# Attention's front end with q and k transposed together, and the first two network parts on their own

## The chip, the cores and the metric

The kernel runs on one core of a Trainium2 chip. The metric is the device time of one execution in microseconds (us); the times of the kernel before are 451.82 us in the median of three runs, from 448.97 to 453.68. Five engines work side by side, each through its own list of instructions in a fixed order: PE (TensorE), DVE (VectorE), ACT (ScalarE), POOL (GpSimd) and SP (SyncE, which here only issues transfers). PEld is PE's loading of weights, which overlaps its matmuls.

## The reference

Three computations follow each other. `x` goes from one to the next, and the result is 768 by 512.

```python
q_bucket = np.sum((q @ proj > 0) * 2 ** np.arange(6), axis=-1)   # k_bucket likewise
scores = np.where(q_bucket[..., :, None] == k_bucket[..., None, :], (q @ k.T) / 8, -1e9)
x = softmax(scores) @ v                # 8 heads, 768 rows, 64 columns per head
idx = np.argmax(x @ w_gate, axis=1)    # 8 experts, 192 slots each, rows beyond them give 0
x = prob[idx] * (relu(x @ w1[idx]) @ w2[idx])          # w1 512x1024, w2 1024x512
h = x @ w_in                           # w_in 512x2048, w_out 2048x512
out = (h * np.tanh(softplus(h))) @ w_out
```

## The kernel before, in words

**Attention.** Rows come in six tiles of 128 (NT). Each head loads q, k and v from three tensors (`ldq`, `ldk`, `ldv`, L593, 192 KB each). So that PE can work on them in fast form, each number is split into a rounded part and what is left of it (hi and lo; `qh kh vh`, L607 to L611, and `ql kl vl`, L619). The hi and lo columns of a row tile lie side by side, so one transpose turns both: 12 transposes per head in four units of three (`t1`, L625), each unit copied out of PSUM by ACT or DVE (`e1`, L630 to L636). 12 matmuls give the hash of each row (`hash`, L653, 12 output columns), and three DVE operations make the bucket number (`bits`, L658, L660, L664). DVE then writes two one-hot blocks of 64 columns, one for q and one for k (`noh`, `oh`, L669). Another 12 transposes turn them together with the lo columns (`t2`, L625), and four more copies take them out (`e2`). Each row tile's scores are four matmuls of 384 columns (L692, L694), in which the one-hot rows add a large negative number wherever the buckets differ. Then come the row maximum (DVE, L700), the exponential (ACT, L708), the transposes of the result (L722), its split (ACT L727, DVE L732), the product with v (L744), its copy out (`ao`), a product that stacks the heads and makes routing logits (`comb`, L755), and the division (L760 to L773). For head 0 the front end stands alone; for each later one it lies between the pieces of the head ahead of it.

**Weights.** They come as float64 in 512 KB pieces into a ring of raw tiles (`wd`, SP, L543). DVE makes them float32 (L552, L554, L559), ACT rounds them (`wh`, L573), and DVE or POOL takes what is left (`wl`, L580). While attention runs, 13 chunks and the zeroing of the slot table (`slots<-zt`, L823) are already issued by SP.

**Experts.** Rows are scattered into the slot table, and each of eight experts does its two products (L1064, L1106) with turns between them. The lo part of the hidden rows is `mhl` (DVE, L1100), the lo part of the result `x2l` (L1145).

**Network.** 16 parts f. Part f has 24 matmuls of 384 columns (L1232), copies `hs` (ACT, L1242), then the activation: `em` (DVE L1249), exponential `e1` (ACT L1252), logarithm `ln` (ACT L1255), `u` (DVE L1258), sigmoid `sg` (ACT L1261), `hm` (DVE L1264), and the split `gh` (ACT L1269), `gl` (DVE L1272). The second product has 18 matmuls of 512 columns per part (L1278). ACT loads a table of functions whenever it goes from one function to the other, and parts are taken in pairs for that: `ln` of an f waits for `e1` of both, `sg` for `u` of both.

**The order.** A planner (class `Planner`) writes every engine's list. It takes tasks with durations, needs and buffers (`attention_tasks`, `expert_tasks`, `network_tasks`), always picks the one that can start earliest (in steps of 0.03 us), and breaks ties by a number per task (`WHEN`, `FIRST` for head 0, `THEN` behind attention). At run time every engine waits for the next instruction of its list.

Of the kernel before, what the change touches and what calls it, by code (L numbers as in the profile page):

```python
# [27 lines left out]
WHEN = dict(idr=142.35, pw=-4386.57, hq=1487.71, wg=-2258.33, ldq=-1065.41, ldk=408.14, ldv=-933.74, qh=4350.55,  # L28
            kh=7076.95, vh=-2343.1, ql=-1970, kl=-1005.3, vl=-1974.29, t1=328.97, e1=-3068.68, hash=-2989.07,
            bits=-3218.52, noh=-1694.11, oh=67.94, t2=-4179.97, e2=-727.14, sc=444.63, max=-637.61, exp=454.86,  # L30
            at=-500.47, hi=-164.99, lo=-592.17, av=548.75, ao=2666.7, iw=93.96, comb=-1492.56, rd=335.58,
            xn=-1105.92, xx=-1665.2, lm=-2664.42, wd=46.84, wh=1211.43, wl=-766.44)
FIRST = dict(idr=-652.1, pw=3097.94, hq=-5268.81, wg=4852.97, ldq=-3302.54, ldk=-4013.68, ldv=-2005.56,
             qh=-1840.12, kh=-619.74, vh=-193.5, ql=674.23, kl=1694.78, vl=1753.74, t1=514.73, e1=-4820.19,
             hash=-1040.76, bits=-3757.41, noh=1020.62, oh=1163.2, t2=-335.62, e2=-12.95, sc=-671.62,
             max=-449.07, exp=-3416.38, at=-1894.24, hi=-3265.28, lo=-59.9, av=55.37, ao=-2910.58, iw=6221.07,
             comb=660.11, rd=2707.9, xn=396.72, xx=-575.46, wd=2263.3, wh=-1337.27, wl=291.71)
# [17 lines left out]

class Task:
# [1269 lines left out]
```

## Time and profile before

| | |
|---|---|
| profiled execution | 450.76 us, of which the span is 449.0 us |
| PE, PEld | 418.1 us (93%), 373.2 us (83%) |
| DVE, ACT, POOL | 348.4 us (78%), 322.8 us (72%), 85.9 us (19%) |
| to the first score matmul | 15.55 us |
| attention to the last stacking product | 137.05 us |
| routing and scatter | 27.40 us |
| experts | 119.50 us |
| network | 144.20 us |

The stages are cut where PE goes over from one to the next, and lie one behind the other. The granted clock is TensorE's, 1.00 being 2.4 GHz and 0.50 being 1.2 GHz. A matmul's own duration overlaps that of the next one, so the distance between starts says what one costs.

### The profile page before, as it was taken

What the parts mean: (1) busy time and instruction counts of PE and PEld (TensorE: products, weight loads), DVE (VectorE), ACT (ScalarE), POOL (GpSimd) and SP (SyncE); (2) the same over time, 40 slices, a digit from 0 to 9 for tenths busy, and PEclk for the clock granted to TensorE, in tenths of its full rate; (3) what the DMA queues carried; (4) which work ended last, traced back from release to release, by engine and by line L of the source; (5) the groups of instructions that cost most, each with busy time, mean ns of one, the idle gap of its engine ahead of it and who ended that gap; (6) DMA issues with size and microseconds to landing.
All of it is one profiled execution on the core that took longest, in us unless ns stands there. A gap on an engine that the chain in (4) does not pass through costs nothing.

```text
span 449.0 us, 7298 instructions
## 1 busy us (share of the span) xinstructions
PE 418.1 (93%) x2630; PEld 373.2 (83%) x2630; DVE 348.4 (78%) x566; ACT 322.8 (72%) x527; POOL 85.9 (19%) x120
## 2 busy tenths in 40 slices
PE   8999999999999985899989899699589999999995
PEld 8989999999999873775767778599578998998884
DVE  6799899898898694191929978999999999964530
ACT  4598897877877634393848887636999799887932
POOL 5966594251000068000000000000000000000005
PEclk8899999999999999899999999989979999999999
DMA  6453345224100057895848999855633351000003
GB/s 185 135 177 108 110 112 169 72 78 136 48 1 0 1 189 153 250 338 212 272 162 267 367 330 311 301 186 188 213 116 130 128 165 47 1 0 2 0 0 140
DMA packets 30136, 65.13 MB, mean 145 GB/s; under 512 B 4752, under 2 KB 7824, under 8 KB 30096
## 3 DMA queue, kind: packets, MB, share of 16 engines
q1 hardware_dynamic: 28944, 61.44, 42.2%
q0 software_dynamic: 1152, 3.16, 1.8%
q8 instruction: 24, 0.39, 0.4%
q14 instruction: 16, 0.13, 0.1%
HBM read 58.26 MB, written 6.33 MB: 144 GB/s over the span
## 4 chain that ended last, share of the span: by engine, by line
issue 57%; POOL 3%; DMA 2%; POOLq 0%; SPq 0%
POOL idd L953 1%; DMA idd<-tokid,pos_i 1%; POOL out_dram L953 1%; DMA ids<-idd 0%; POOL apart L952 0%; POOLq L1321 0%; POOL slots L953 0%; POOLq L953 0%; SPq L968 0%
## 5 line engine op out<-in xcount | busy, mean ns | idle before, releaser
L580 DVE TENSOR_TENSOR wl<-raw,wh 128x1024 fp32r<-128x1024 f32 (+1 forms) x90 | 89.8, 1029 | 17.2 <-ACT wh L573 17.0
L573 ACT CAST wh<-raw 128x1024 fp32r<-128x1024 f32 (+1 forms) x96 | 85.8, 925 | 4.9 <-DVE raw L559 3.5
L953 POOL DMA_INDIRECT out_dram<-osb,ids x6 | 5.8, 962 | 260.5 <-ACT osb L1284 260.5
L700 DVE TENSOR_REDUCE nm<-ps 128x1 f32<-128x768 f32 x48 | 45.5, 951 | 5.6 <-PE ps L694 5.3
L732 DVE TENSOR_TENSOR atl<-pt,ath 128x512 fp32r<-128x512 f32 x72 | 46.7, 684 | 3.6 <-ACT ath L727 3.5
L708 ACT ACTIVATE a<-ps,nm 128x768 f32<-128x768 f32 x48 | 44.0, 918 | 3.7 <-DVE nm L700 3.6
L727 ACT CAST ath<-pt 128x512 fp32r<-128x512 f32 x72 | 39.1, 595 | 6.8 <-PE pt L722 6.5
L1232 PE MATMUL pg<-x2h,wh 128*128 128x384 f32 x128 | 44.0, 344 | 0.0
L1232 PE MATMUL pg<-x2l,wh 128*128 128x384 f32 x128 | 43.8, 342 | 0.0
L1232 PE MATMUL pg<-x2h,wl 128*128 128x384 f32 x128 | 43.7, 341 | 0.0
L1278 PE MATMUL po<-wh,gh 128*128 128x512 f32 x96 | 38.5, 401 | 5.5 <-ACT gh L1269 5.5
L1278 PE MATMUL po<-wh,gl 128*128 128x512 f32 x96 | 38.5, 401 | 0.9 <-DVE gl L1272 0.9
L722 PE MATMUL pt<-identf,a 128*128 128x128 f32 x288 | 38.7, 275 | 0.2 <-ACT a L708 0.2
L1278 PE MATMUL po<-wl,gh 128*128 128x512 f32 x96 | 38.4, 400 | 0.0
L744 PE MATMUL pa<-ath,vn 128*128 128x256 f32 x144 | 37.4, 295 | 0.5 <-ACT ot L632 0.5
L744 PE MATMUL pa<-atl,vn 128*128 128x256 f32 x144 | 35.5, 282 | 0.0
L722 PEld LDWEIGHTS pt<-identf,a 128*128 128x128 f32 x288 | 32.1, 141 | 1.6 <-ACT a L708 0.5
L1106 PE MATMUL py<-wh,mhl 128*128 128x512 f32 (+1 forms) x72 | 27.7, 384 | 3.0 <-DVE mhl L1100 3.0
L1106 PE MATMUL py<-wh,mhh 128*128 128x512 f32 (+1 forms) x72 | 27.9, 387 | 0.9 <-PEq L1166 0.6
L1064 PE MATMUL ph<-wh,xh 128*128 128x512 f32 x64 | 26.8, 419 | 1.1 <-PEq L1166 0.4
L744 PEld LDWEIGHTS pa<-ath,vn 128*128 128x128 f32 x144 | 27.2, 189 | 0.7 <-ACT ot L632 0.7
L692 PE MATMUL ps<-xk 128*128 128x384 f32 x96 | 27.3, 365 | 0.0
(197 smaller groups left out, 1015.8 us busy)
## 6 DMA issues: line engine op xcount, KB each, us to landing
raw<-in_moe_w_dram SPq DMA_DIRECT2D x64, 512.0 KB, 5.0
raw<-in_moe_w_in_dram SPq DMA_DIRECT2D x16, 512.0 KB, 4.2
raw<-in_moe_w_out_dram SPq DMA_DIRECT2D x16, 512.0 KB, 3.7
slots<-zt SPq DMA_DIRECT2D x12, 258.0 KB, 4.5
xs<-slots SPq DMA_DIRECT2D x8, 258.0 KB, 5.2
rq<-in_q_dram SPq DMA_DIRECT2D x8, 192.0 KB, 3.1
rk<-in_k_dram SPq DMA_DIRECT2D x8, 192.0 KB, 2.7
rv<-in_v_dram SPq DMA_DIRECT2D x8, 192.0 KB, 2.4
```

The lines of the kernel that those rows point to most:

```text
L573: nc.scalar.copy(out=wt[c][0][:, sl], in_=val)
L580: eng_of[eng].tensor_tensor(out=wt[c][1][:, sl], in0=val, in1=f32(wt[c][0][:, sl]), op=ALU.subtract)
L692: nc.tensor.matmul(ps[:, j, :HW], lhsT=d["xk1"][:, i, :], rhs=xkt[:, j * HW:(j + 1) * HW], start=True, stop=False)
L700: r = nc.vector.tensor_reduce(out=nm, in_=d["ps", i][:, :, :HW], axis=AX.XY, op=ALU.max, negate=True)
L708: nc.scalar.activation(out=a, in_=d.pop(("ps", i))[:, :, :HW], func=AF.Exp, bias=d["nm", i], accum_out=d["rs"][:, i:i + 1])
L722: nc.tensor.transpose(pt[:, j, :], a[:, kt * P:(kt + 1) * P], identf)
L727: nc.scalar.copy(out=d["ath", g][:, sl, :], in_=d["pt", g, u])
L732: nc.vector.tensor_tensor(out=d["atl", g][:, sl, :], in0=d["pt", g, u], in1=f32(d["ath", g][:, sl, :]), op=ALU.subtract)
L744: nc.tensor.matmul(d["pa", g], lhsT=d["vn"][:, kt, :], rhs=mv, start=(kt == 0 and n == 0), stop=(kt == NT - 1 and n == 1))
L1106: nc.tensor.matmul(py[:m, cols], lhsT=ht[j // 2][st][:, 2 * (j % 2) + i, :m], rhs=mv[:, i, cols], start=(j == 0 and i == 0 and n == 0), st ...
L1232: mm = nc.tensor.matmul(pg[:, :HW], lhsT=st[:, kt, fs], rhs=mv[:, kt, j * HW:(j + 1) * HW], start=(kt == 0 and i == 0), stop=(kt == KD - 1 ...
L1278: nc.tensor.matmul(po[t], lhsT=st, rhs=mv[:, f % 2, :], start=(f == 0 and i == 0), stop=(f == NF - 1 and i == 2))
```

## The change

- **One input.** q, k and v are joined along their columns into `qkv`; one transfer per head brings 590 KB (`ld`).
- **One set of transposes.** `turn_qk` (`tq`) turns the raw q and k columns of a row tile in one float32 transpose, 6 per head. q lands on partitions 0 to 63, k on 64 to 127. ACT scales and rounds (`eh`), DVE takes the lo part (`el`), twice each for halves of 384 columns.
- **Hash on the turned side.** Two units of three matmuls 12x384 (`hash`), two comparisons with zero (`bits`, 12 partitions), two matmuls with a constant 12x128 matrix of bucket codes (`cd`), and two comparisons with a threshold (`ev`), which write the one-hot rows of q and k, already turned.
- **Moves.** The scores need q's and k's parts on matching partitions. Five copies per head bring them there: `mk`, `ml`, `mq`, `mo`, `mn`. For head 0 ACT and DVE make them; for heads 1 to 7 they are transfers from SBUF to SBUF on SP, 64 partitions of 3 KB each (196 KB; `mk` writes 393 KB).
- **Gone** are `ql kl qh kh`, `t1 e1`, the two bucket reductions, `noh oh`, `t2 e2`.
- **Codes.** Nine small DVE operations, a transpose and a copy make the code matrix at the start. The transpose stands behind head 0's row transposes.
- **Network.** Parts 0 and 1 are no longer a pair; the later ones still are.
- **Planner.** New durations and new numbers in all three tables.

```diff
+WHEN = dict(ao=13414.87, at=13539.91, av=16012.23, bc=-9226.94, bd=-5917.08, bits=-10160.96, bt=-2431.12,
...
-SLOTS = dict(t=3, s=2, pa=1, a=5, ab=2, qn=2, kn=2, vn=3, x1=2, x2=2, rq=2, rk=2, rv=2)
+SLOTS = dict(t=3, s=2, pa=1, a=5, ab=2, vn=3, x1=3, rq=2, hb=1, hot=2)
...
+        add(("ld", h), {"SP": 0.6}, takes=["rq"], lag=2.0)
...
+        for u in range(2):
+            add(("tq", h, u), {"PE": 0.33}, [("ld", h), ("idr", 0)], ["t"], (), 0.4 * u)
+            add(("eh", h, u), {"ACT": 0.51}, [("tq", h, u)] + [("eh", h, 0)] * u, ["x1"] * (u == 0), (), 0.4 * u)
+            add(("el", h, u), {"DVE": 0.54}, [("eh", h, u)], (), ["t"], 0.4 * u)
+        near = h < 1
+        lag = 0.0 if near else 6.0
+        add(("mk", h), {"DVE": 0.85} if near else {"SP": 0.5}, [("eh", h, 1)], lag=lag)
+        add(("ml", h), {"ACT": 0.8} if near else {"SP": 0.5}, [("el", h, 1)], lag=lag)
+        for u in range(2):
+            add(("hash", h, u), {"PE": 0.52}, [("el", h, u), ("hq", 0)], ["t"], (), 0.4 * u)
+            add(("bits", h, u), {"DVE": 0.46}, [("hash", h, u)] + [("bits", h, 0)] * u, ["hb"] * (u == 0), ["t"], 0.4 * u)
+            add(("cd", h, u), {"PE": 0.2}, [("bits", h, u), ("bd", 0)], ["t"], ["hb"] * u, 0.4 * u)
+            add(("ev", h, u), {"DVE": 0.59}, [("cd", h, u)] + [("ev", h, 0)] * u, ["hot"] * (u == 0), ["t"], 0.4 * u)
+        add(("mq", h), {"DVE": 0.45} if near else {"SP": 0.5}, [("ml", h), ("hash", h, 1)], lag=lag)
+        hot = [("ev", h, 0), ("ev", h, 1), ("mk", h)]
+        add(("mo", h), {"DVE": 0.45} if near else {"SP": 0.5}, hot, lag=lag)
+        add(("mn", h), {"ACT": 0.8} if near else {"SP": 0.5}, hot, lag=lag)
...
-        pair = [("e1", x) for x in ((f - f % 2, f - f % 2 + 1) if f < NF - 2 else (f,))]
+        pair = [("e1", x) for x in ((f - f % 2, f - f % 2 + 1) if 2 <= f < NF - 2 else (f,))]
...
+    def turn_qk(h, u, eng):
+        pt = hd[h]["tq", u] = ps_t.tile([P, NT // 2, P], F32, tag="t", name="ptq")
+        for j in range(NT // 2):
+            nc.tensor.transpose(pt[:, j, :], hd[h]["rq"][:, u * NT // 2 + j, 0:2 * D], identf)
...
+        nc.scalar.activation(out=half(d["xq"], 1, u), in_=d["tq", u].rearrange("p t c -> p (t c)"), func=AF.Copy, scale=scol)
...
+        nc.vector.scalar_tensor_tensor(out=half(d["xq"], 0, u), in0=d["tq", u].rearrange("p t c -> p (t c)"), scalar=scol,
+                                       in1=f32(half(d["xq"], 1, u)), op0=ALU.mult, op1=ALU.subtract)
...
+        for n, (w, i) in enumerate(((hw_h, 1), (hw_l, 1), (hw_h, 0))):
+            nc.tensor.matmul(ph[:2 * NB, :], lhsT=w, rhs=half(d["xq"], i, u), start=(n == 0), stop=(n == 2))
...
+        nc.vector.tensor_scalar(out=d["hb"][:, u * HW:(u + 1) * HW], in0=d["ph", u][:2 * NB, :], scalar1=0.0, scalar2=None, op0=ALU.is_gt)
...
+        nc.tensor.matmul(pc, lhsT=code, rhs=d["hb"][:, u * HW:(u + 1) * HW], start=True, stop=True)
...
+        nc.vector.tensor_scalar(out=d["hot"][:, u * HW:(u + 1) * HW], in0=d["cd", u], scalar1=thr, scalar2=hot,
+                                op0=ALU.is_gt, op1=ALU.mult)
```

PE's list at the front end of head 6, between pieces of head 5 (`ptm` are the front end's transposes, `ph` the hash, `ps` scores, `pt` transposes of the exponentials, `pc` the stacking). Before, the four hash and transpose units, and behind a gap the second set of transposes:

```order
L625 MATMUL ptm<-identr,qn 128x128 x3
L692 MATMUL ps<-xk_1451 128x384 x2
L694 MATMUL ps<-xk_1560 128x384 x2
L653 MATMUL ph<-hq,xk_1710 128x12 x6
L625 MATMUL ptm<-identr,kn 128x128 x6
...
L653 MATMUL ph<-hk,xk_1710 128x12 x6
...
L625 MATMUL ptm<-identr,qn 128x128 x6
L755 MATMUL pc<-iw,ot 128x72 x6
L625 MATMUL ptm<-identr,kn 128x128 x6
```

Of the change (`ptq` transposes of raw q and k, `ph` the hash, `pcd` the codes):

```order
L708 MATMUL ps<-xk,xq 128x384 x4
L682 MATMUL ph<-xq,hw_h 12x384
L682 MATMUL ph<-xq,hw_l 12x384
L682 MATMUL ph<-xq,hw_h 12x384
L633 MATMUL ptq<-identf,rq 128x128 x3
...
L694 MATMUL pcd<-hb,code 128x384
L737 MATMUL pt<-identf,a 128x128 x4
...
L770 MATMUL pc<-iw,ot 128x72 x6
L694 MATMUL pcd<-hb,code 128x384
```

24 transposes and 12 hash matmuls of a head have become 6 transposes, 6 hash matmuls and 2 for the codes. SP's list in the same place, with the moves of head 6 (L652), in which a weight load and a piece of the zeroing stand between the first two moves and the other three:

```order
L652 DMA xk<-xq 64x2x768
L652 DMA xk<-xq 64x768
L550 DMA raw<-in_moe_w_dram 128x2x512
L861 DMA slots<-zt 128x516
L652 DMA xq<-hot 64x768
L652 DMA xk<-hot 64x768
L652 DMA xq<-xq 64x768
```

Before, the lines of that place held only loads, weights and zeroing. DVE's list at the last expert, before (`mhl` is what the second product waits for):

```order
L552 TENSOR_SCALAR full<-raw 128x512
L554 SCALAR_TENSOR_TENSOR raw<-raw,full 128x512
L559 SCALAR_TENSOR_TENSOR raw<-raw 128x512
L1145 ISA
L1145 TENSOR_TENSOR x2l<-px,x2h 128x4x128
L559 SCALAR_TENSOR_TENSOR raw<-raw 128x512
L580 TENSOR_TENSOR wl<-raw,wh 128x512
L1100 TENSOR_TENSOR mhl<-px,mhh 128x512
L580 TENSOR_TENSOR wl<-raw,wh 128x512
L1100 TENSOR_TENSOR mhl<-px,mhh 128x512
```

and of the change:

```order
L559 TENSOR_SCALAR full<-raw 128x512
L561 SCALAR_TENSOR_TENSOR raw<-raw,full 128x512
L1136 TENSOR_TENSOR mhl<-px,mhh 128x512 x2
L1181 ISA
L1181 TENSOR_TENSOR x2l<-px,x2h 128x4x128
```

Both `mhl` now stand ahead of `x2l` and of the last steps of the weights, and no `wl` stands between them. ACT's list in the network from the exponential to the first `gh`, before:

```order
L1252 ACTIVATE e_g<-e_g 128x768
L1242 COPY hs_g<-pg 128x384
L1255 ACT_TABLE_LOAD
L1255 ACTIVATE e_g<-e_g 128x768
L1242 COPY hs_g<-pg 128x384
L1255 ACTIVATE e_g<-e_g 128x768
L573 CAST wh<-raw 128x512 x2
L1252 ACT_TABLE_LOAD
L1252 ACTIVATE e_g<-e_g 128x768
L1261 ACT_TABLE_LOAD
L1261 ACTIVATE e_g<-e_g 128x768 x2
L1269 CAST gh<-hs_g 128x768 x2
```

and of the change, from the first exponential on:

```order
L1288 ACTIVATE e_g<-e_g 128x768
L1278 COPY hs_g<-pg 128x384
L1291 ACT_TABLE_LOAD
L1291 ACTIVATE e_g<-e_g 128x768
L1278 COPY hs_g<-pg 128x384 x2
L1297 ACT_TABLE_LOAD
L1297 ACTIVATE e_g<-e_g 128x768
L1278 COPY hs_g<-pg 128x384
L580 CAST wh<-raw 128x512
L1278 COPY hs_g<-pg 128x384
L1305 CAST gh<-hs_g 128x768
```

The logarithm of part 0 now stands behind its own exponential, and no table of the exponential is loaded between it and the sigmoid. PE's list in the network goes with that: 96 matmuls L1232 (parts 0 to 3) stand ahead of the first L1278 instead of 120 (parts 0 to 4).

## Rows read from the trace of the kernel before

**Rows 1.** Windows by stage; columns: stretch, length, busy time and instructions per engine, clock, DMA share.

```profile
0.00:15.55 15.55, 13.98 (x127) 13.62 (x127) 9.76 (x29) 6.02 (x11) 9.63 (x33) 0.78 0.60 168
15.55:152.60 137.05, 135.34 (x1124) 132.60 (x1124) 121.10 (x211) 110.21 (x233) 53.77 (x51) 1.00 0.30 90
...
299.50:443.70 144.20, 137.82 (x673) 123.58 (x672) 112.37 (x174) 113.92 (x153) 4.75 (x9) 0.98 0.26 89
```

**Rows 2.** Windows by head period in the attention stage, columns as in rows 1.

```profile
98.54:115.71 17.17, 17.17 (x146) 17.07 (x145) 15.29 (x29) 13.61 (x30) 2.12 (x2) 1.00 0.30 94
```

**Rows 3.** Waits of DVE, 40 to 140 us: total, times, longest.

```profile
DVE nm L700 <- PE ps L694: 4.0, 8, 0.7
```

**Rows 4.** Timeline of weight loads: start, length, instruction; each matmul has one load.

```profile
80.35 0.31 PEld L692 LDWEIGHTS ps<-xk 128*128 128x128 f32 x2
80.65 0.36 PEld L694 LDWEIGHTS ps<-xk 128*128 128x128 f32 x2
81.00 1.40 PEld L722 LDWEIGHTS pt<-identf,a 128*128 128x128 f32 x12
82.36 0.30 PEld L692 LDWEIGHTS ps<-xk 128*128 128x128 f32 x2
...
86.08 0.81 PEld L653 LDWEIGHTS ph<-hq,xk 128*128 128x128 f32 x6
86.83 0.57 PEld L625 LDWEIGHTS ptm<-identr,kn 128*128 128x128 f32 x6
87.35 0.30 PEld L692 LDWEIGHTS ps<-xk 128*128 128x128 f32 x2
```

**Rows 5.** Groups by line, attention stage: count, then shortest, median, longest ns, then starts.

```profile
L658 DVE TENSOR_REDUCE hs<-ph x7: 297/298/298, 17.4 to 123.6; 128x72 f32<-128x144 f32 x7
L660 DVE SCALAR_TENSOR_TENSOR hb<-hs,pow x7: 232/232/1007, 17.7 to 123.9; 128x72 f32<-128x72 f32 x7
L664 DVE TENSOR_REDUCE bk<-hb x7: 228/228/228, 18.1 to 124.2; 128x12 f32<-128x72 f32 x7
L669 DVE TENSOR_TENSOR kn<-cols,bk x7: 549/957/1114, 22.5 to 126.1; 128x384 fp32r<-128x384 f32 x7
L634 DVE TENSOR_SCALAR xk<-ptm x7: 548/558/559, 27.2 to 120.0; 128x384 fp32r<-128x384 f32 x7
```

**Rows 6.** The page's DMA issues: count, KB each, median us from issue to landing.

```profile
raw<-in_moe_w_dram SPq DMA_DIRECT2D x64, 512.0 KB, 5.0
...
rv<-in_v_dram SPq DMA_DIRECT2D x8, 192.0 KB, 2.4
```

**Rows 7.** Timeline of DVE at the last expert.

```profile
288.74 0.68 DVE L1145 TENSOR_TENSOR x2l<-px,x2h 128x512 f32 x1
...
290.54 0.68 DVE L1100 TENSOR_TENSOR mhl<-px,mhh 128x512 fp32r<-128x512 f32 x1
```

**Rows 8.** Timeline of PE at the last expert and in the network.

```profile
291.28 0.58 PE L1106 MATMUL py<-wh,mhl 128*128 128x256 f32 x1 [3.03 <-DVE mhl L1100]
...
318.12 0.34 PE L1232 MATMUL pg<-x2h,wh 128*128 128x384 f32 x1
318.30 0.34 PE L1232 MATMUL pg<-x2l,wh 128*128 128x384 f32 x1
...
326.45 0.79 PE L1278 MATMUL po<-wh,gh 128*128 128x512 f32 x1 [5.52 <-ACT gh L1269]
```

**Rows 9.** Windows of two half-clock stretches, columns as in rows 1.

```profile
292.00:294.00 2.00, 2.00 (x11) 2.00 (x10) 1.82 (x4) 0.00 (x0) 0.00 (x0) 0.50 0.87 295
...
326.00:332.00 6.00, 4.69 (x12) 3.69 (x13) 5.97 (x10) 5.77 (x9) 0.00 (x0) 0.50 0.21 73
```

**Rows 10.** Timeline of ACT in the network.

```profile
320.25 1.28 ACT L1252 ACT_TABLE_LOAD   x1
```

**Rows 11.** Groups by line, DVE in the network: count, busy us, mean ns.

```profile
L580 DVE TENSOR_TENSOR wl<-raw,wh 128x512 fp32r<-128x512 f32 x28 | 18.9, 685 | 0.0
...
L1272 DVE TENSOR_TENSOR gl<-hs_g,gh 128x768 fp32r<-128x768 f32 x16 | 14.9, 954 | 5.6 <-ACT gh L1269 5.6
```

More of the change, by code (lines that the diff above doesn't have):

```diff
@@ L270, in convert @@
             add(("cb", c, i), {"DVE": 0.62}, [("ca", c, i)], when=at)
[L271 removed]
+            add(("wh", c, i), {"ACT": 0.55}, [("cb", c, i)] + ([("wh", c, 0)] if i else before), [place] * (i == 0), when=at)
             add(("wl", c, i), {"DVE": 0.62}, [("wh", c, i)], (), ["raw"], at)
@@ L615, in part_lo, with load @@
[L615 to L626 removed]
+    def load(h, eng):
+        hd[h]["rq"] = nat.tile([P, NT, 3 * D], F32, tag="rq", name="rq")
+        nc.sync.dma_start(out=hd[h]["rq"], in_=qkv[0, h].rearrange("(p t) d -> p t d", t=NT))
@@ new lines, in _body, with v_hi @@
+    eng_of = {"DVE": nc.vector, "Pool": nc.gpsimd}
+    def v_hi(h, eng):
+        vn = hd[h]["vn"] = nat.tile([P, NT, 2 * D], F32R, tag="vn", name="vn", bufs=3)
+        out, src = vn[:, :, 0:D], hd[h]["rq"][:, :, 2 * D:3 * D]
+        if eng == "ACT":
+            nc.scalar.copy(out=out, in_=src)
+        elif eng == "DVE":
+            nc.vector.tensor_copy(out=out, in_=src)
+        else:
+            nc.gpsimd.tensor_tensor(out=out, in0=src, in1=ones[:, :D].unsqueeze(1).to_broadcast([P, NT, D]), op=ALU.mult)
@@ new lines, in move, with move_k, move_l @@
+    def move(out, in_, eng):
+        if eng == "SP":
+            nc.sync.dma_start(out=f32(out), in_=f32(in_))
+        elif eng == "ACT":
+            nc.scalar.copy(out=out, in_=f32(in_))
+        else:
+            nc.vector.tensor_copy(out=out, in_=f32(in_))
+    def move_k(h, eng):
+        d = hd[h]
+        move(d["xk"][0:D, :, :], d["xq"][D:P, 1, :].unsqueeze(1).to_broadcast([D, 2, S]), eng)
+    def move_l(h, eng):
+        d = hd[h]
+        move(d["xk"][D:P, 0, :], d["xq"][D:P, 0, :], eng)
@@ L648, in prep_hash, with move_q, move_o, move_n @@
+    def move_q(h, eng):
+        d = hd[h]
+        move(d["xq"][D:P, 0, :], d["xq"][0:D, 1, :], eng)
+    def move_o(h, eng):
+        d = hd[h]
+        move(d["xk"][D:P, 1, :], d["hot"][0:D, :], eng)
+    def move_n(h, eng):
+        d = hd[h]
+        move(d["xq"][D:P, 1, :], d["hot"][D:P, :], eng)
     def prep_hash(h, u, eng):
         d = hd[h]
-        if u == 0:
-            d["ph"] = ps_t.tile([P, 2 * NT, 2, NB], F32, tag="t", name="ph")
-        for t in range(3 * u, 3 * u + 3):
-            nc.tensor.matmul(d["ph"][:, t], lhsT=d["xk1"][:, t, :], rhs=hq if t < NT else hk, start=True, stop=True)
@@ L1311 @@
     arrays, args = {}, []
+    inputs = dict(inputs, qkv=_np.concatenate([inputs[x] for x in "qkv"], axis=-1))
     for name in _INS:
```

279 lines of the change are left out of this document (119 added, 160 removed).

## Prediction

> **What bounds the kernel now.** I read the stages first [rows 1]. From the first score matmul at 15.55 us to the last stacking product PE is busy 135.34 of 137.05 us at full clock, so attention is bound by PE, and work taken off PE there is worth its length. A head period in the middle of it shows what comes next [rows 2]: 17.17 us, PE in all of it, PE's weight loads 17.07, DVE 15.29, ACT 13.61, POOL 2.12, and the four periods that I read agree within 0.02. DVE is thus only 1.9 us behind PE. Its waits are mostly for PE, 4.0 us in 8 waits of score matmuls over 100 us [rows 3]. In the network PE is busy 137.82 of 144.20 us [rows 1], and its idle time is nearly one wait: 5.52 us for the first split activation [rows 8], after which the granted clock is 0.50, the lower level (1.2 GHz) [rows 9]. At the last expert PE waits 3.03 us for `mhl` [rows 8].
>
> **Attention, PE.** Distances between starts of weight loads give what a matmul costs when PE is full [rows 4]: the four of a score tile 0.65 (80.35 to 81.00, 0.163 each), twelve float32 transposes 1.36 (81.00 to 82.36, 0.113 each), six hash matmuls 0.75 (86.08 to 86.83, 0.125 each), six of the front end's transposes 0.52 (86.83 to 87.35, 0.087 each). A head loses 24 x 0.087 + 12 x 0.125 = 3.6 us. It gains 6 x 0.113 = 0.7 for the transposes of raw q and k, and eight matmuls of 384 columns, six for the hash and two for the codes. The trace has none with 12 output columns or 12 rows; the score matmul has the same 384 columns, 0.163, and the 12-column hash matmul at 0.125 is the lower bound. I take 0.163: 1.3. Net -1.6, from 17.2 to 15.6 us per head.
>
> **Attention, DVE.** A head loses the three bucket operations, 0.30 + 0.23 + 0.23, two one-hot blocks, 0.55 at the least and 0.96 in the median of `kn` [rows 5], and 18 of the 64 copies of all heads, 2.25 x 0.56: 3.5 us. It gains two `el`, two `bits`, two `ev`, each 384 elements a partition out of PSUM; the nearest row is the copy of that size, 0.56 [rows 5], so up to 3.35. DVE then stands at about 15.1 against PE's 15.6. Nothing on DVE was slack in its list: with 0.5 us instead of 1.9 to spare, rows wait for DVE that did not before. I take 1.1 of the 1.6 us, for seven heads, **-8**. Ends: -10.5 if every wait still fits, -3 if DVE sets the pace at 16.7.
>
> The spread of `kn`, 549 to 1114 ns for the same shape [rows 5], has a reason in the Trainium skill, page "SBUF — State Buffer", section "SBUF: two separate sides": a DVE operation with two SBUF inputs and a GpSimd operation that reads SBUF shut each other out for a whole instruction. The trace agrees so far that `kn` has two SBUF inputs and that POOL splits heads in the same stretch. By that rule `kn`'s own cost is 0.55 and 0.4 us per head of what I took off DVE was time behind POOL, which goes too since POOL also loses the splits of q and k; the sum would be the same.
>
> **ACT and POOL.** ACT loses 46 of those 64 copies, 5.75 per head, and gains two `eh`; POOL loses the four splits of q and k. Both were behind PE already [rows 2], so I cost them at nothing.
>
> **The moves.** Five transfers per head for heads 1 to 7 lie on SP and in PE's way: PE cannot start a head's scores before they land. No row shows a transfer from SBUF to SBUF. The nearest is v's load, 192 KB in 2.4 us; a 512 KB weight piece takes 5.0 in the busier mean [rows 6]. Between a head's last codes matmul and its first score matmul PE's new list has other work, which I summed with the distances above: 8.2 us at head 1, 8.3 at head 6, 10 to 13 at the others. Out of it go a comparison on DVE, 0.56 and its queue there, SP's issue behind a weight piece and a zeroing piece, and the landing. With 2.4 to 5.0 that is 4 to 7, under the cover, so I cost the moves at 0; the lower end is 0 too (they replace no transfer), the upper end is rival 3. The joined load is one issue instead of three, early enough to be hidden except at head 0.
>
> **The start.** Nothing covers head 0's front end: DVE is busy 9.76 of 15.55 us [rows 1] and waits in between for ACT, PE and loads. In the new list DVE has 14 operations between the landing of the joined load and the first score, most of 384 elements; the one of 1536 I count as two: 15 x 0.56 [rows 5] = 8.4 us. The load is 590 KB; between v's 2.4 and the 5.0 of 512 KB [rows 6] plus 0.7 until it is issued I take 4.7, and 0.4 for the first transpose and `eh`: 13.5, **-2**. Ends: +0.5, if the load takes 6 and one more wait shows, and -3.5. The nine operations for the codes stand ahead of the landing.
>
> **The last expert.** Before, `x2l` at 288.74 and three more operations at 0.6 apart stand ahead of `mhl` at 290.54 [rows 7]; PE waits until 291.28 [rows 8]. In the new list both `mhl` stand ahead of these four: 4 x 0.6 = 2.4 us earlier. The wait shrinks to some 0.6, and the half clock behind it [rows 9], eleven matmuls in 2 us, may shrink with it. **-2.5**, from -1 (the second `mhl` is late, or the weights' last steps, now behind it, are) to -4.
>
> **The network.** 384 matmuls L1232 at 0.177 (318.12 to 318.30 [rows 8]) are 67.8 us. Lost are 5.52, some 0.9 for `gl` behind it, and at half clock 12 matmuls in 5.1 us (326.45 to 332.00 less 0.5 [rows 8, 9]) that would take 2.3 at full clock, so 2.4 more: 8.8 in all. In the new list PE needs the first `gh` after 96 matmuls, 17 us, instead of 120, 21 us; part 0's activation waits neither for part 1 nor for the exponential's table load of 1.28 [rows 10]. But DVE makes `gl`, and what stands ahead of it there is mostly weights: adding its list at the durations of the trace less their overlap (0.60 for each of the weights' steps, 0.86 for `gl` and its like, from 0.685 and 0.954 [rows 11]) puts `gl` of part 0 at 16 to 17 us, that of part 1, which stands behind three activations at once, at 33. PE wants part 1 at 17 + 9 x 0.235 + 48 x 0.177 + 9 x 0.235 = 29.6. So about 1 us of wait at part 0, 3.5 at part 1, and some 1.5 of half clock behind it, as behind the 3.03 us at the last expert: 6 of 8.8 stay lost. **-3**, from 0 to -7.
>
> **The rest** (routing, the seven other experts, the tail) is the same work in a new order: 0, give or take 3.
>
> **Sum.** -8 - 2 - 2.5 - 3 = -15.5 from the profiled execution's 450.76: 435.3. That execution stands 1.06 below the median of the runs, inside their spread, so against the median it is 436.3; I predict **436 us**. 1%, 4.5 us, is about what a measurement of this kernel can tell from no change.
>
> **Rivals.**
> 1. *DVE becomes the bound.* For it: 15.29 of 17.17 [rows 2], and six new operations from PSUM. Against: it is waiting for PE now [rows 3]. Period 16.7 to 17: attention gives 2 instead of 8: 442. Chance 0.20.
> 2. *All fits.* PE stays as full as it is and DVE hands `gl` of part 1 over in time: -10.5 in attention and -6 in the network give -21 in place of -15.5, less 3 for a neighbour that is late: 427 to 430. Chance 0.12.
> 3. *The moves land late: slower than before.* Place: the first score of each of heads 1 to 7. It costs from the point where they take over 8 us from the codes matmul; over 10.4 (15.5 / 7 = 2.2 per head more) the gain is gone; at 11.3, 3.3 us seven times is 23 us: 458. For it: SP issues in order, and at head 6 a weight piece that needs a free raw tile and a zeroing piece stand ahead of the last three moves; if that tile is late, so are the scores. Against: DMA is at 0.30 of its time in attention [rows 1], and v's load lands in 2.4 [rows 6]. Chance 0.06. The Trainium skill speaks for it: page "SBUF — State Buffer", section on the DMA port swizzle, says that a transfer on partitions 0 to 63 or 64 to 127 reaches half the ports; by it a move would take an estimated twice the transfer time of a full one. No run here shows it.
> 4. *Unpairing only moves the wait* from part 0 to part 1, and the network stays at 144: the change would not do there what it says. For it: DVE's sum above. 438 to 440. Chance 0.08.
>
> The forecast itself, 430 to 441, has 0.54. Slower by over 1% is rival 3: 0.06. Within 1%, from 447.3 to 456.3, are the upper tails of rivals 1 and 4 and of the forecast: 0.08. Faster takes 0.86. The range 426 to 447 leaves out rival 3, those tails and a low end of rival 2, together under 0.2.
>
> **What would show it.** Head periods near 16.1 us, PE full or with short waits for DVE, and DVE over 0.92 of them; a first score matmul near 13.5; no wait of `ps` for a DMA at heads 1 to 7; at the last expert under 1 us for `mhl`; in the network two waits, the larger at the second product of part 1, and 141 us. The prediction is wrong if `ps` waits for moves in every head, if the new matmuls cost well over 0.163, or if the replanned experts lose what attention gives.

## The result

The change makes the kernel a little faster: 449.23 us in the median of 16 runs against 451.58 in 16 runs of the kernel before beside it, a ratio of 0.9916 with a 95% interval of 0.9887 to 0.9945. The ratios in this document are taken over fast runs alone and so are not the quotients of the medians (here 0.9948): three of the 16 runs were slow, one of them 515.99 us long at a mean clock of 0.75. I had forecast 436 us and a range of 426 to 447. The sign is right, the size is not, and the time lies outside the range. The profiled execution took 444.37 us (span 442.6), 4.9 below its kernel's median; the one of before stands 0.8 below its own. So 9.1 us of the 13 that are missing can be read from the trace of after (444.37 against the 435.3 of the sum), and some 4 us to what differs between executions.

The stages, read from PE's instructions, in us; attention and network are cut as before, what lies between them otherwise. "Scatter" runs from the last stacking product to the first product of expert 1, and so holds routing, scatter and expert 0; "experts" goes from there to the end of the last expert's first product, and "to the network" holds that expert's second one.

| kernel | first score | attention | scatter | experts | to the network | network |
|---|---|---|---|---|---|---|
| before | 15.55 | 137.0 | 30.7 | 97.0 | 19.2 | 144.25 |
| after | 15.00 | 134.7 | 28.5 | 99.2 | 18.6 | 141.4 |
| change | -0.55 | -2.3 | -2.2 | +2.1 | -0.5 | -2.9 |

The windows of after in some of these stages, and in the last row from the division of head 1 (`rd`) to that of head 7; columns are stretch, length, busy time and instructions of PE, PEld, DVE, ACT and POOL, granted clock, DMA share, GB/s:

```profile
0.00:15.00 15.00, 11.39 (x103) 8.62 (x104) 12.35 (x42) 6.25 (x9) 9.29 (x33) 1.00 0.53 151
15.00:149.70 134.70, 130.54 (x957) 120.11 (x956) 118.26 (x197) 99.28 (x205) 24.14 (x20) 0.99 0.56 155
...
296.00:437.40 141.40, 138.16 (x673) 123.18 (x672) 113.76 (x176) 110.37 (x152) 4.82 (x9) 0.98 0.29 100
46.92:142.76 95.84, 94.72 (x712) 88.79 (x712) 87.88 (x149) 72.69 (x154) 14.84 (x11) 1.00 0.53 149
```

They answer to [rows 1, 2]. From the division of head 1 to that of head 7, six heads on, it takes 95.84 us. PE is busy in 94.72 of them, and DVE for a share of 0.92. A sixth is 15.97 us, which looks like the 16.1 of my forecast, but the stretch does not hold six front ends. The new list has the transposes of three heads ahead of the first score, and this stretch has 24 of them, 24 hash matmuls (four heads' worth of each) and 9 codes matmuls. The same window for the instructions on `ptq` alone, then on `pcd` alone (the columns begin with PE, PEld and DVE):

```profile
46.92:142.76 95.84, 3.87 (x24) 2.78 (x24) 4.89 (x8) 4.54 (x8) 1.00 0.53 149
46.92:142.76 95.84, 3.94 (x9) 1.63 (x9) 6.05 (x9) 1.00 0.53 149
```

A whole head is better added up from the mean distances between starts of weight loads in this stretch: 24 score matmuls at 0.169, 36 transposes of exponentials at 0.120, 36 products with v at 0.125, 12 stacking products at 0.113, 6 transposes of q and k at 0.110, 6 hash matmuls at 0.172 and 2 for the codes at 0.368 make 16.66 us. This is an estimate; the same sum for the kernel before gives 17.3, where 17.17 was measured [rows 2]. So a head became some 0.5 us cheaper and not 1.1, and the stage got 2.3 us shorter, not 8. From the first score to the division of head 1 it takes 31.9 us instead of 29.1. From head 7's division to the end it takes 6.9 instead of 5.6, but there 58 instructions of PE stand behind that marker instead of 45, so this alone is no loss.

The weight loads at the codes, as they stand between a score tile and transposes of the exponentials (start, length, instruction, idle time before it and who ended it):

```profile
96.41 0.66 PEld L708 LDWEIGHTS ps<-xk,xq 128*128 128x128 f32 x4
97.32 0.18 PEld L694 LDWEIGHTS pcd<-hb,code 12*128 12x128 f32 x1 [0.25 <-DVE nm L715]
97.69 0.42 PEld L737 LDWEIGHTS pt<-identf,a 128*128 128x128 f32 x4 [0.19 <-issue]
```

This answers to [rows 4]. The load of the 12-row code matrix starts 0.25 us after the score tile's last load has ended, and the next starts 0.37 after it. A score matmul costs 0.163 [rows 4]. What the new operations take on DVE, against [rows 5] (count, busy us, mean ns, idle before them):

```profile
L700 DVE TENSOR_SCALAR hot<-pcd,thr,hot 128x384 fp32r<-128x384 f32 x13 | 8.7, 671 | 2.7 <-PE pcd L694 2.6
L647 DVE SCALAR_TENSOR_TENSOR xq<-ptq,scol,xq 128x384 fp32r<-128x384 f32 x12 | 7.3, 609 | 0.6 <-ACT xq L643 0.4
L688 DVE TENSOR_SCALAR hb<-ph 12x384 fp32r<-12x384 f32 x12 | 6.4, 536 | 0.5 <-PE ph L682 0.4
```

PE's waits in the order of time, which answer to [rows 8]: head 3's first transposes, a product of the experts behind the handling of rows that don't fit, the last expert, and the network.

```profile
19.92 0.52 PE L633 MATMUL ptq<-identf,rq 128*128 128x128 f32 x3 [2.04 <-DMA rq<-in_qkv_dram]
202.63 0.43 PE L1083 MATMUL px<-identf,xs 64*128 64x64 f32 x4 [1.85 <-DVEq L1188]
289.76 0.39 PE L1142 MATMUL py<-wh,mhl 128*128 128x256 f32 x1 [1.95 <-issue]
328.81 0.79 PE L1314 MATMUL po<-wh,gh 128*128 128x512 f32 x1 [2.88 <-ACT gh L1305]
```

The first and the second have no counterpart of that length before: one is a wait of the new order for the joined load, in whose wake the clock falls, the other is 0.43 us there. The windows around the first of them, and around the second, show what follows (columns as above):

```profile
20.00:22.00 2.00, 2.00 (x12) 1.64 (x13) 0.68 (x1) 0.00 (x0) 0.00 (x0) 0.83 0.90 258
22.00:24.00 2.00, 2.00 (x10) 1.93 (x9) 1.63 (x3) 0.78 (x2) 0.00 (x0) 0.50 0.95 359
...
200.00:204.00 4.00, 1.65 (x13) 0.93 (x10) 2.31 (x4) 1.90 (x5) 0.00 (x0) 1.00 0.83 300
204.00:208.00 4.00, 4.00 (x19) 2.36 (x18) 0.00 (x0) 0.00 (x0) 0.00 (x0) 1.00 0.02 6
```

After the wait at head 3 the clock is 0.83 and then 0.50, the lower level (1.2 GHz). In the experts PE is busy in 1.65 of 4 us, but in this execution the clock stayed at 1.00.

### The profile page after: what moved, and what is told of

Same layout as the page of the kernel before. It is cut to its first block, busy times and chain, and to the rows that moved or that the text cites. A ratio compares the mean times of both kernels' runs of the same rounds, so it can differ in the third digit from the quotient of the medians.

```text
span 442.6 us, 6927 instructions
## 1 busy us (share of the span) xinstructions
PE 410.3 (93%) x2440; PEld 354.9 (80%) x2440; DVE 348.6 (79%) x565; ACT 307.2 (69%) x495; POOL 54.6 (12%) x90
## 4 chain that ended last, share of the span: by engine, by line
issue 57%; POOL 3%; DMA 2%; POOLq 0%; SPq 0%
POOL idd L989 1%; DMA idd<-tokid,pos_i 1%; POOL out_dram L989 1%; DMA ids<-idd 1%; POOL apart L988 0%; POOLq L1358 0%; POOL slots L989 0%; POOLq L989 0%; SPq L1004 0%
## 5 line engine op out<-in xcount | busy, mean ns | idle before, releaser
L587 DVE TENSOR_TENSOR wl<-raw,wh 128x1024 fp32r<-128x1024 f32 (+1 forms) x90 | 88.4, 1030 | 11.1 <-ACT wh L580 9.7
L580 ACT CAST wh<-raw 128x1024 fp32r<-128x1024 f32 (+1 forms) x96 | 83.6, 923 | 5.3 <-DVE raw L566 2.7
L708 PE MATMUL ps<-xk,xq 128*128 128x384 f32 x192 | 44.1, 356 | 0.2 <-ACT a L723 0.2
L737 PEld LDWEIGHTS pt<-identf,a 128*128 128x128 f32 x288 | 33.9, 143 | 3.1 <-DVE atl L747 1.4
L708 PEld LDWEIGHTS ps<-xk,xq 128*128 128x128 f32 x192 | 32.5, 192 | 2.4 <-ACT a L723 1.2
```

The costliest lines, as they stand in the source:

```text
L580: nc.scalar.copy(out=wt[c][0][:, sl], in_=val)
L587: eng_of[eng].tensor_tensor(out=wt[c][1][:, sl], in0=val, in1=f32(wt[c][0][:, sl]), op=ALU.subtract)
L708: nc.tensor.matmul(ps[:, j, :HW], lhsT=d["xq"][:, i_, i * P:(i + 1) * P], rhs=half(d["xk"], i_, j), start=(i_ == 0), stop=(i_ == 1))
L737: nc.tensor.transpose(pt[:, j, :], a[:, kt * P:(kt + 1) * P], identf)
```

## Experiments

The expectations name their theories by letters. A: a codes matmul with few weight rows costs far more than a full one; B, its rival: DVE is the next limit, and cheaper codes give nothing. C: head 3's early transposes cost the wait and the half clock behind it. G: the new order of the experts costs what the trace of after doesn't show in full. Each timed run has its own runs of the kernel before beside it, so I compare ratios: the unchanged kernel was timed twice, 0.9916 and 0.9936, in the mean 0.9926, and one per cent of before is 4.5 us. An interval of some 0.006 to either side makes a difference of under 3 us uncertain. The profiled executions lie closer together than the medians: 444.37 and 445.46 us for the unchanged kernel, each the shortest of its runs, and 441.32 to 445.30 for the five versions below that are faster. So the traces can place only a part of what the times gain.

### The code matrix and the bits padded to 128 rows

```diff
-    code = const.tile([2 * NB, P], F32R, name="code")
+    code = const.tile([P, P], F32R, name="code")
-            d["hb"] = sm.tile([2 * NB, S], F32R, tag="hb", name="hb", bufs=1)
+        d["hb"] = hball                     # [128, 768], zeroed once, rows 0 to 11 written per head
```

> The changed kernel with the two codes matmuls of a head on 128 weight rows in place of 12 (the rows beyond 12 are zeros, zeroed once at the start); everything else, and every list, is as in the changed kernel. Theory A (a matmul with 12 weight rows makes PE run dry before and behind it: 0.37 us from its start to the next one's and some 0.2 us ahead of it, where 0.163 was reckoned): the distance falls to 0.16 to 0.18, the gap ahead of it goes, PE's list between first score and last stacking product gets some 5 us shorter, the time falls by 4 to 5.5 us against the changed kernel (ratio to the kernel before from 0.992 to 0.980 to 0.983). Rival B (DVE is the next bound): the gaps at the codes matmul go, but PE waits for DVE instead, and the time falls by under 1.5 us.

Measured: 443.39 us, ratio 0.9768 [0.9707, 0.9828], 1.58% or 7.1 us less than after (5.8 between the medians), more than expected. The weight loads of this kernel in the same place:

```profile
95.06 0.66 PEld L707 LDWEIGHTS ps<-xk,xq 128*128 128x128 f32 x4
95.70 0.19 PEld L693 LDWEIGHTS pcd<-hball,code 128*128 128x128 f32 x1
95.88 0.53 PEld L736 LDWEIGHTS pt<-identf,a 128*128 128x128 f32 x4
```

The gap ahead is gone and the next load comes 0.18 later: from the score tile's first load to the load behind the codes it takes 0.82 us instead of 1.28. Of the 16 codes matmuls 13 stand behind the first score. Over these the distance to the next load is 0.36 to 0.38 in after and 0.11 to 0.24 here, 0.37 and 0.17 in the mean, and the idle time ahead is 0.18 in the mean and next to none here. From the load ahead of the codes to the load behind them it takes 0.72 us in the mean in after and 0.31 here: 0.41 us for each matmul, 5.3 us for the 13. The stretch from the division of head 1 to that of head 7:

```profile
47.35:140.08 92.73, 91.60 (x712) 88.75 (x711) 87.10 (x148) 72.55 (x154) 14.91 (x11) 1.00 0.56 154
```

It holds the same instructions of PE as in after and is 3.1 us shorter, of the 3.7 that its 9 codes matmuls should give. A whole head, added up as above, is 16.04 us, at the 16.1 of the forecast, and DVE is at 0.94 of the stretch. A holds for the matmul and what stands around it, and B falls: DVE was no bound. But attention as a whole takes 132.0 us, 2.7 less than in after, where I expected some 5: in the first heads the four codes matmuls there give nothing, and the wait for head 3's load is 2.79 us instead of 2.04. The rest of what the time gained I can't place; the scatter stage of this profile is even 3.2 us longer.

### Codes with 64 rows

```diff
-        nc.tensor.matmul(pc, lhsT=code, rhs=d["hb"][:, u * HW:(u + 1) * HW], ...)
+        nc.tensor.matmul(pc, lhsT=code[:64, :], rhs=d["hb"][:64, u * HW:(u + 1) * HW], ...)
```

> The codes matmul on 64 weight rows, the rest zeros, otherwise as on 128 rows. Theory A in its wider form (any matmul on fewer than 128 weight rows between full ones makes PE run dry): 0.37 us from its start to the next, as on 12 rows. In its narrow form (only the short one): 0.17, as on 128.

One run, 447.77 us, too few for a verdict on the time, but the trace answers. Weight loads of this kernel:

```profile
100.13 0.18 PEld L693 LDWEIGHTS pcd<-hball,code 64*128 64x128 f32 x1 [0.25 <-DVE nm L714]
100.50 0.42 PEld L736 LDWEIGHTS pt<-identf,a 128*128 128x128 f32 x4 [0.19 <-issue]
```

64 rows cost the same 0.37 and the same gap as 12. It isn't the 12 that is dear but the change between 128 weight rows and fewer, or the fewer themselves.

### Head 3's first transposes later in PE's list

```diff
+    plan = planner.run(attention_tasks(H, NT, WA, RAW), fill=FILL)
+    late_tq = plan.pop(next(i for i, x in enumerate(plan) if x[0] == ("tq", 3, 0)))
+    plan.insert(next(i for i, x in enumerate(plan) if x[0] == ("eh", 3, 0)), late_tq)
```

> The changed kernel with one thing moved in PE's list: the first three transposes of head 3, which stand early in head 0's stretch and wait 2.04 us for that head's joined load, stand right ahead of the ACT operation that reads them. Theory C (this wait and the half clock behind it cost the start of attention some 4 us): the wait is gone, the granted clock stays 1.00 from 15 to 30 us, and the time falls by 3 to 4.5 us (ratio 0.982 to 0.985). Rival D (head 0's stretch is a chain through DVE and ACT, whatever PE does): PE waits for DVE's one-hot rows or row maxima in the same place, the time falls by under 1 us.

Measured: 445.34 us, ratio 0.9822 [0.9768, 0.9877], 4.7 us less than after (3.9 between the medians). The windows in this kernel:

```profile
20.00:22.00 2.00, 1.77 (x12) 1.50 (x11) 2.00 (x4) 1.81 (x4) 0.00 (x0) 1.00 0.97 219
22.00:24.00 2.00, 2.00 (x17) 1.67 (x15) 2.00 (x4) 1.96 (x5) 0.00 (x0) 1.00 0.91 293
```

The clock stays at 1.00 from 15 to 30 us, and PE does 17 instructions in 22 to 24 us where after does 10. Attention takes 132.4 us, 2.3 less than in after. C holds, with the time at the upper end of its forecast, of which this stage shows about half.

### Both

> Both edits together. Theories A and C: the gains add, 7 to 10 us less than the changed kernel (ratio 0.970 to 0.977), attention from first score to last stacking product some 126 to 128 us. Rivals B and D: under 3 us together, with PE waiting for DVE in most heads.

The edits of the two runs together: 442.91 us, ratio 0.9764 [0.9706, 0.9823], 7.3 us less than after (6.3 between the medians), where the singles sum to 11.8. They don't add up. With the first heads faster, other waits appear there (PE's waits in this kernel: line waited for, total, times, longest):

```profile
PE ps L707 <- ACT a L722: 1.3, 3, 0.5
PE ps L707 <- DMA xq<-xq: 1.3, 1, 1.3
```

Attention is 129.1 us here, above the 126 to 128 expected of both edits, but 7.9 below before, which is what the prediction had forecast for it. The scatter stage takes 32.5 instead of 28.5 and gives 4 of these back.

### Parts 0 and 1 as a pair again

```diff
-        p = begin + 7.8 * (f - f % 2) if 2 <= f < NF - 2 else b
+        p = begin + 7.8 * (f - f % 2) if f < NF - 2 else b
```

(and likewise in `pair` and `both`)

> The changed kernel with the first two network parts taken as a pair again, as before (the same planner numbers). If the network's 2.9 us came from unpairing: the network takes 144 us again with one wait of over 5 us for the first gh, time 2.5 to 3.5 us longer than the changed kernel (ratio 0.998 to 1.000). Rival: it came from the other planner numbers, then the network stays at 141 to 142 and the time at 0.992.

Measured: 454.53 us, ratio 1.0049 [1.0011, 1.0087], 5.6 us above after, more than expected. The network takes 146.85 us instead of 141.4. PE in this kernel:

```profile
333.04 0.80 PE L1314 MATMUL po<-wh,gh 128*128 128x512 f32 x1 [8.76 <-ACT gh L1305]
```

The long wait for the first split activation is back, and is longer than before [rows 8], since the rest of the plan was made for unpaired parts. So in this plan the unpairing is worth more than the whole 2.9 us, and without it the change would be slightly slower than before. What a plan made anew for paired parts would take isn't tested.

### The unchanged kernel again

> The changed kernel once more, unchanged, for a second profile and an interval beside the others of this call. Its profiled execution took 444.4 us, the median of its 16 runs is 449.2. Theory E (executions differ in how late transfers land: the joined loads, the expert rows behind the scatter, PE's instructions): this profile shows the same work with longer waits for transfers, 447 to 451 us. Rival: the profiled execution was no exception in its waits and the runs differ in the clock alone; then the waits add up to the same and only the half-clock stretches are longer.

Measured: 448.71 us, ratio 0.9936 [0.9903, 0.9969]; its profiled execution took 445.46, below the 447 to 451 of Theory E. PE's waits for the experts' rows add up to 5.8 us, as in the first profile. The windows of that execution from the gap in the experts on:

```profile
200.00:204.00 4.00, 1.66 (x12) 1.13 (x10) 2.18 (x4) 1.90 (x5) 0.00 (x0) 0.84 0.84 310
204.00:208.00 4.00, 4.00 (x10) 2.05 (x10) 0.12 (x1) 0.00 (x0) 0.00 (x0) 0.50 0.03 7
177.94:280.66 102.72, 95.07 (x446) 72.29 (x445) 67.23 (x73) 68.86 (x95) 0.00 (x0) 0.97 0.73 261
```

The same program and the same gap, but here the clock falls to 0.50 behind it and PE does 10 instructions in 204 to 208 us instead of 19. The experts take 102.72 us instead of 99.16. At the last expert it is the other way round; the stage from the experts to the network in this execution, and then in the first one of after:

```profile
280.66:297.59 16.93, 13.65 (x89) 11.67 (x88) 16.14 (x26) 8.13 (x14) 0.00 (x0) 1.00 0.63 220
```

```profile
277.35:296.00 18.65, 15.30 (x89) 13.32 (x88) 16.89 (x26) 8.32 (x14) 0.00 (x0) 0.91 0.58 204
```

Here the clock is 1.00 all through, there 0.91, and the stage is 1.7 us longer with the same 89 matmuls. An execution with both of these falls would take 444.4 + 3.6 = 448.0 us, near the median; that the median runs are such is worked out, not seen, since both profiled executions are the fastest of their runs. The mean granted clock of every run speaks for it, and for the rival of Theory E: it is 0.982 to 0.983 in the runs of 444.37, 446.18 and 447.08 us of after and 0.968 to 0.978 in those from 447.26 to 450.56, and here 0.982 in the run of 445.46 and 0.964 in those of 451.25 and 451.70. From 0.983 to the 0.975 in the median is an estimated 3.5 us of 443, if PE were the bound all through.

### The experts in the order of before

The tie-breaking numbers of the experts' tasks (`THEN` for `oo xs xd l1 re ht hh hl l2 ga xg yt yh yl xt xh xl wd wh wl dm ca cb`) go back to those of before; attention and network stay as in after.

> The changed kernel with the planner's numbers of the kernel before for the experts' tasks and their weights (23 of the numbers behind attention); PE's list in the experts is then that of the kernel before, the network keeps part 0 on its own. Theory G (the new expert order puts the turns of expert 1's hidden rows ahead of the overflow branch; PE then waits 1.8 us for DVE's branch with nothing left to do, is busy 1.65 of 4 us there, and in many executions runs 2.7 to 4 us at half clock behind it): PE is busy over 3.4 of the 4 us at that branch at clock 1.00, expert 1 to the end of the last first product takes 97 to 98 us instead of 99 to 103, and the time falls by 2 to 4 us against the changed kernel (ratio 0.984 to 0.988). Rival H (the experts are held by the stream of weights): the distance stays at 99 to 103 and the time within 1 us.

Measured: 444.86 us, ratio 0.9857 [0.9819, 0.9896], 3.1 us less than after (4 between the medians); the interval just touches one of the two of after. The windows of this kernel:

```profile
200.00:204.00 4.00, 2.97 (x15) 1.62 (x14) 0.42 (x1) 0.37 (x1) 0.00 (x0) 1.00 0.96 380
204.00:208.00 4.00, 4.00 (x19) 2.44 (x18) 0.00 (x0) 0.54 (x1) 0.00 (x0) 1.00 0.02 6
180.31:277.99 97.68, 91.46 (x446) 70.44 (x445) 66.27 (x72) 67.97 (x95) 0.00 (x0) 1.00 0.82 277
```

PE is busy in 2.97 of the 4 us (over 3.4 were expected), the clock stays up, and the experts take 97.7 us instead of 99.2 and 102.7 in the two profiles of after. G holds for that stage, and in the time as far as 3 us can be told. The profiled execution as a whole took 445.30 and is no shorter than those of after: its scatter stage takes 31.2 us. The numbers went back together, so which of them opens the gap isn't told apart.

### Part 2 alone as well, on top of the two attention edits

```diff
-        add(("e1", f), {"ACT": 0.77}, [("em", f)], (), (), p + 12, table="e")
+        add(("e1", f), {"ACT": 0.77}, [("em", f)] + [("sg", 1)] * (f == 2), (), (), p + 12, table="e")
```

> Codes on 128 rows, head 3's transposes late, and one more need in the planner: the exponential of network part 2 waits until part 1 has its sigmoid, so that part 1 has logarithm and sigmoid tables of its own. Theory F (the wait that is left in the network is part 1's gh, held up by the tables and DVE work of parts 2 and 3): that wait falls from 3.0 us to under 1, the network from 142 to 138 or 139 us, 3 us less than with the first two edits (ratio 0.969 to 0.972). Rival: DVE is the limit; the wait comes back at part 2, and the time stays or rises by up to 2 us.

Measured: 451.24 us, ratio 0.9997 [0.9967, 1.0028], 2.3% or 10.5 us above the run with both edits (8.3 between the medians). PE in this kernel:

```profile
328.56 0.79 PE L1317 MATMUL po<-wh,gh 128*128 128x512 f32 x1 [3.59 <-ACT gh L1308]
344.08 0.50 PE L1317 MATMUL po<-wh,gh 128*128 128x512 f32 x1 [3.73 <-ACT gh L1308]
```

F fails: the wait for part 1's `gh` is 3.59 us instead of 3.0 with both edits, and a new one of 3.73 stands at part 2. The network takes 150.4 us instead of 142.5. The rival has the place of the new wait right, and more is lost than it forecast.

### All three repairs

Padded codes, the later transposes of head 3, and the experts' old order.

> The codes on 128 rows, head 3's transposes late, and the experts' old numbers, in one kernel. Theories A, C and G: 439 to 441 us (ratio 0.970 to 0.975), 2 to 4 less than with the first two. Rival H: 443, as with the first two.

Measured: 441.69 us, ratio 0.9786 [0.9750, 0.9821]. It beats before and after, but not the versions with padded codes: 0.9768, 0.9764 and 0.9786 can't be told apart. The three singles (7.1, 4.7, 3.1) sum to 14.9 us, more than the whole miss, but together they give 6.3 (7.5 between the medians). The wait that grows is the one for the experts' rows out of the slot table. In this kernel, and then in after:

```profile
PE px L1073 <- DMA xs<-slots: 7.2, 3, 5.7
```

```profile
PE px L1083 <- DMA xs<-slots: 5.8, 3, 2.6
```

The scatter stage takes 31.8 us here and 28.5 in after. It is 30.8 to 32.5 in all six versions with repairs, 28.0 and 28.5 in the two profiles of after, and 28.5 with 64 code rows. But it is also 31.1 with the pairs, 31.2 with the experts' old order alone, and 30.7 in the kernel before, where attention ends at most 0.6 us earlier than in after, or later, so an early end of attention doesn't explain it. POOL writes the slot table in six instructions. The fifth of them in after, and then in the version with the experts' old order alone:

```profile
163.40 0.96 POOL L989 DMA_INDIRECT slots<-x_nat,slot_i  x1 [0.19 <-issue]
```

```profile
162.78 2.03 POOL L976 DMA_INDIRECT slots<-x_nat,slot_i  x1 [0.19 <-issue]
```

It takes 0.96 us in the three profiles with the short stage and 2.03 in the eight others. The first load of the experts' rows is issued 17.9 to 18.9 us behind the last stacking product in the three, at 19.0 in before, and at 20.9 to 21.8 in the other seven. So 2 to 4 us of what the faster versions gain ahead of this stage are lost in it. The long write goes with that, but in before the load follows it about as early as in after, so it is not the whole cause. Why it takes longer, and whether it does in every execution of a version, is open.

## Why the prediction was wrong

**The start (-2): 0.55 came.** First scores stand at 14.9 to 16.2 us in all the runs, never at 13.5. The load was not late: what waits for it goes on at 4.18, where I took 4.7 for the landing. DVE's 14 operations also cost what I took, 0.56 from start to start. What I left out stands ahead of and behind them. In after (start, length):

```profile
4.18 0.36 DVE L608 CAST vn<-rq 128x384 fp32r<-128x384 f32 x1 [0.64 <-DMA rq<-in_qkv_dram]
5.16 0.17 DVE L804 CAST phi<-pw 128x6 fp32r<-128x6 f32 x1 [0.62 <-DMA pw<-in_proj_dram]
...
6.54 0.60 DVE L647 SCALAR_TENSOR_TENSOR xq<-ptq,scol,xq 128x384 fp32r<-128x384 f32 x1
...
13.23 0.55 DVE L656 CAST xk<-hot 64x768 fp32r<-64x768 f32 x1
13.64 0.83 ACT L654 CAST xq<-hot 64x768 fp32r<-64x768 f32 x1
14.75 0.50 PE L633 MATMUL ptq<-identf,rq 128*128 128x128 f32 x3
15.00 0.94 PE L708 MATMUL ps<-xk,xq 128*128 128x384 f32 x4
```

DVE waits 0.62 us for the projection's load and does that work before its first `el`, which starts 2.36 us behind the landing. Behind its last copy, done at 13.78, come a copy on ACT and transposes of head 2 on PE, 1.2 us to the first score. 1.45 us of the miss.

**The heads (-8): 2.3 came.** Two steps failed here. The first is the price of the new matmuls: "I take 0.163", with 0.125 as the lower bound. For the six of the hash it was about right (0.17 to 0.19 between their starts). The codes matmuls took 0.37, and a gap ahead: 0.41 us each above the same matmul on 128 rows, 5.3 us in the stage. I had bounded them from shapes of 128 rows on one side and 12 output columns on the other; no row of before showed fewer than 128 weight rows in that place, and I gave that unknown no upper end, though "well over 0.163" is among my own signs of being wrong. A whole head shows it: 16.66 us, and 16.04 with padded codes, where I had 15.6 from PE's list and 0.5 for DVE.

The second is the cover of the joined load. I wrote that it is "early enough to be hidden except at head 0". Head 3's first transposes stand in PE's list ahead of a load that had not landed, and the 2.04 us wait plus half clock contradict me; setting them later gave 4.7. That load was issued at 12.99 and PE went on at 19.92:

```profile
12.99 1.06 SPq L598 DMA_DIRECT2D rq<-in_qkv_dram  x1
```

That is 6.9 us, where I took 4.7 for a joined load. With both steps set right (the run with both edits) attention is 7.9 us shorter than before, as forecast, though new waits of some 2.6 us are in it, so that an agreement this close is partly luck.

The page of after would have hidden this. Its DMA issues (KB each, median us from issue to landing) give 4.4 us for the joined load, and 4.7 for the largest move:

```profile
rq<-in_qkv_dram SPq DMA_DIRECT2D x8, 576.0 KB, 4.4
...
xk<-xq SPq DMA_DIRECT2D x7, 384.0 KB, 4.7
```

But of the eight joined loads in that trace only one has its landing on record. In the second profile of the unchanged kernel all eight have it:

```profile
DMA to landing us min/median/max: 3.5/5.4/6.9
```

On the codes, the Trainium skill speaks for my price: in the page "TensorE: Matmul & The Clock Gate", section "Why this matters for your kernels", a single matmul with 32 rows takes the same time as one with 128, and in "Step-by-step: what each phase is for" the row count doesn't matter to a weight load. The trace agrees for the load itself, 0.18 us with 12 rows and 0.19 with 128. It does not for what stands around it: 0.41 us more for each such matmul among full ones with 12 rows, and the same distance and gap with 64. The measurement decides.

**The moves (0) and rival 3: right.** No `ps` waits for a move in after. In three of the faster versions one does, once, for 0.75 to 1.25 us.

**ACT, POOL and DVE's bound: right.** From the division of head 1 to that of head 7 ACT is busy in 72.69 of 95.84 us and POOL in 14.84. Rival 1 did not happen: DVE is at 0.94 of that stretch with padded codes, PE is busy in 91.60 of its 92.73 us, and PE is still the bound.

**The last expert (-2.5): 0.5 came in the profile.** The move did what the list says:

```profile
284.69 1.28 DVE L1136 TENSOR_TENSOR mhl<-px,mhh 128x512 fp32r<-128x512 f32 x2
285.89 0.68 DVE L1181 TENSOR_TENSOR x2l<-px,x2h 128x512 f32 x1
```

Both `mhl` now stand ahead of `x2l`, the reverse of [rows 7], and PE doesn't wait 3.03 us for them. But the same PE instruction stands still for 1.95 us for nothing that the profile shows, and then the clock falls. In the second profile of the unchanged kernel the wait is there as well (1.85) and the clock stays up, and the stage gave 19.16 - 16.93 = 2.2 us. So the term was about right where the clock held, and the half clock that I had seen behind the old wait [rows 9] can also follow the new one. What PE waits for there is open. In each of the five profiles with this wait a transfer of 16 KB on an instruction queue starts 0.2 to 0.6 us ahead of it, but such transfers also lie where PE doesn't wait. In the five other versions the wait doesn't appear, but there PE waits 2.0 to 2.6 us for ACT's `ysb` just ahead of the network, so that this stage is hardly shorter there (16.6 to 17.2 us) than where the wait stood and the clock held (16.9).

**The network (-3): 2.9 came.** As argued, the 5.52 us wait is gone and one of 2.88 us is left, for part 1's activation and not part 0's: the first `gh` is handed over in time. Rival 4 did not happen, and the run that pairs the parts again shows that in this plan the unpairing is needed for it. One difference in my sum was off: 5.1 less 2.3 is 2.8 and not 2.4, so 9.2 us and not 8.8 were to be had; the -3 is hardly touched by it.

**The rest (0, give or take 3):** in the profiled execution the scatter's -2.2 and the experts' +2.1 cancel, and the first of these goes with POOL's fifth write (0.96 us here, 2.03 before), which the change doesn't touch. That the sum was right is thus luck. But the old experts' order makes the kernel 3 to 4 us faster, so the "same work in a new order" had a price, at the edge of the bound that I gave it. Part of it is paid only in executions whose clock falls behind the gap, and the first profile of after is not one.

So of the 13 us, the profile holds 1.45 (start), 5.7 (heads), 2.0 (last expert) and nothing (network and rest), together 9.1; the remaining 4 are what its median stands further above its profile than I had allowed for (4.9 instead of 1.06). The range failed because it had no end for the price of the codes nor for a joined load that lands late behind head 0, and took the new order of everything behind attention at a small, even risk.

## What to carry to other kernels

Before a matmul with fewer than 128 weight rows goes between full ones, try it padded with zeros: here that took 0.41 us off each of them, made the whole kernel 6 to 7 us faster, of which the trace shows 2.7 in attention, and cost one zeroed tile. A new order has to be read for its earliest loads and for places where several engines meet, since a wait of 2 us there can be paid twice, once as it is and once as half clock behind it. When a period is read off a trace, the instructions in it have to be counted: here a stretch of six heads held the front ends of four. And gains that were each shown alone need not add up: the next wait (here the slot table's rows) takes its share.

## What the runs showed of the hardware

- A matmul with 12 or 64 weight rows among ones with 128 costs about 0.41 us more than one with 128 rows, 0.20 behind its load and 0.21 ahead, though its own load takes the same 0.18 us (13 matmuls with 12 rows and 13 padded ones; with 64 rows one run).
- Around one and the same gap (PE busy in 1.65 and 1.66 of 4 us) the clock is 1.00 in one execution and 0.84, then 0.50, in another of the same program; the experts take 3.6 us longer with it.
- A wait of PE of 1.7 to 2.3 us appears in five profiles at the same instruction of the last expert, with no releaser in the trace, and is absent in the five others.
- The fifth of six writes of the slot table on POOL takes 0.96 us in three profiles and 2.03 in eight; the other five take 0.95 to 1.21 in all of them.
- Joined loads of 576 KB landed 3.5 to 6.9 us behind their issue in one execution, the longest beside moves and weight pieces at a DMA share of 0.95 from 15 to 30 us.
